# Layer 1 of experts 1 to 7 over two chunks of tokens at a time, and an earlier order of the first attention rounds

## The chip, the cores and the metric

The kernel runs on one core of one Trainium2 chip. The metric is the device time of one execution in microseconds. It was taken four times before the change: 698.27, 698.76, 696.95 and 697.79 us, median 698.03 us. The profile is of one execution, of 698.27 us.

Engines go by these names: PE multiplies matrices (PEld is its loading of the stationary operand), DVE, ACT and POOL work on vectors, SP only issues transfers. ACT and POOL issue transfers too. Each engine takes its instructions in the order of its own queue.

## The reference

Two parts, one behind the other: attention, whose output (reshaped) is the input x of a mixture of experts with a Sinkhorn weighting.

```python
# attention: batch 4, heads 8, sequence 768, head size 64
scores = scale * np.matmul(q, k.transpose(0, 1, 3, 2))
mask = np.where(is_retrieval, causal, causal & (is_sink | in_window))
a = softmax(np.where(mask, scores, -1e9))
x = np.matmul(a, v).transpose(0, 2, 1, 3).reshape(3072, 512)
# mixture: 8 experts, 512 -> 1024 -> 512
P = np.exp(x @ w_gate - max)
for _ in range(8):
    P /= P.sum(1, keepdims=True) + 1e-09
    P /= P.sum(0, keepdims=True) + 1e-09
    P *= N / E
for e in range(8):
    out += P[:, e:e + 1] * (np.maximum(x @ w1[e], 0.0) @ w2[e])
```

## The kernel before

**First phase, attention.** Work comes in units (batch b, 256 query rows g, four heads u). For each unit the keys and queries are transposed on PE (`emit_prep`, lines 271 and 277, with a DVE copy into kT at line 284), scores are made (`emit_scores`, line 476), ACT takes the exponential into PT (line 485), DVE masks PT (lines 494 and 497), PE multiplies with v (`gen_pv`, line 313), DVE normalizes into xn (lines 326 and 327), and PE and ACT turn the result into xT, the transposed x (`turn`, lines 342 and 345). Expert 0 is computed in between, as fillers (lines 383 and 397), as soon as 256 columns of xT are there. In the first batch, v arrives in another order of rows and is put in place by a small matmul against the identity (`gen_place_v`, line 136) and two copies, one by ACT (line 145) and one by DVE (line 143).

For PE, DVE and ACT the order of this phase is written out by hand. The first six rounds stand in the code one by one (lines 551 to 607); from the seventh on it is a loop. `warm(n)` issues n matmuls of 512 columns whose results nobody reads (line 299).

**Second phase.** Eight Sinkhorn steps on DVE with a tiny matmul each (line 645), and the rest of the fillers.

**Third phase, experts 1 to 7.** The 3072 tokens are six chunks of 512. The list `works` has 42 entries (expert e, chunk c). Both layers use a Strassen-Winograd scheme: each operand is cut into 2 x 2 blocks, seven products of blocks take the place of eight, and sums and differences of blocks are made beforehand on DVE (`left` for the stationary side, line 708, and `right` for the moving side, line 717), four per operand.

- `combine_w(e)` makes S1 from w1 and T2 from w2, `combine_x(c)` makes T1 from one chunk of x (cut into two halves of 256 tokens), `combine_h(e, c)` makes S2 from h.
- `layer1(e, c)` computes h for one chunk. The 1024 hidden features are cut into two halves of 512, and each half into two column groups g of 2 x 128. One product of one group is four matmuls of 256 moving columns (line 771) into a bank of PSUM. Several products are added up in the same bank "y", and between them ACT copies the bank to R (line 780). DVE adds R to another bank with a relu (line 786), and ACT ends the last block with a relu (line 810). There are four such banks.
- `layer2(e, c)` makes seven products of eight matmuls each (line 836), which are weighted with the gate and added to acc: products 1, 5, 6 and 7 by DVE (line 853), products 2, 3 and 4 by ACT into a tile (line 850) and an accumulating transfer issued by POOL (line 858). In the last two entries all are added by DVE.
- The first entry uses a plain layer 1 (`layer1_plain`, line 751: 32 matmuls of 512 columns), the last a plain layer 2 (`layer2_last`, line 888).

`body(n)` runs over the entries. In it, seven slots each issue two products of layer 1 for entry n and one product of layer 2 for entry n - 1, with the combinations of weights, x and h in given slots. At its end it makes the first two combinations of h for entry n. The order of DVE is by hand (line 943); that of PE, ACT, POOL and SP comes from a scheduler, from what the code emits. h lies in a pool of two buffers (line 743). The weights of the next expert are loaded at its predecessor's first chunk, w1 (line 157) and w2 (line 162) one after the other. Finished blocks are stored from SP's queue (line 822).

Of the kernel before, what the change touches and what calls it, by code (L numbers as in the profile page):

```python
# [3 lines left out]

# [6 lines left out]
F32 = mybir.dt.float32  # L11
# [25 lines left out]
def kernel(  # L37
# [88 lines left out]
    def place_v(g):  # L126
        run(gen_place_v(g), 2)

    def gen_place_v(g):

        parts = []
        for n in range(2):
            t = psA.tile([128, 512], F32, tag="mo", bufs=3, name=f"vp_{g}_{n}")
            rows = slice(64 * n, 64 * n + 64)
            for c in range(2):
                nc.tensor.matmul(
                    out=t[64 * c:64 * c + 64, :].rearrange("p (h d) -> p h d", h=H),
                    lhsT=ident16[rows, rows], rhs=vraw[g][rows, :, c, :], start=True, stop=True,
                )
            parts.append((v_tile(0)[:, :, 2 * g + n, 0:D], t.rearrange("p (h d) -> p h d", h=H)))  # L140
        for n, (dst, src) in enumerate(parts):
            if g == 2 or n:
                nc.vector.tensor_copy(out=dst, in_=src)
            else:
                nc.scalar.activation(out=dst, in_=src, func=AF.Copy, bias=0.0, scale=1.0)
            yield
# [403 lines left out]
    with tc.manual_schedule(engines=engines):  # L550
# [10 lines left out]
        make_masks((2,))  # L561
        emit_prep(*preps.pop())
        warm(2)
        soften(r0, (1,))
        r1 = scores(1)
        r1[0][0]()
        place = gen_place_v(0)
        run(place, 1)
        r1[1][0]()
        sum_later(0)  # L570
        emit_prep(*preps.pop())
        run(place, 1)
        finish_sums()
        make_masks((3,))
# [3 lines left out]
        place_v(1)  # L578
        turn()
        sum_later(1)  # L580
        r3 = scores(3)
        finish_sums(lambda: emit_prep(*preps.pop()))
# [3 lines left out]
        sum_later(2)  # L586
        r4 = scores(4)
        turn()
# [71 lines left out]

    CH = 512
# [58 lines left out]
    def combine_w(e):  # L720
        w1, w2 = expw[e]
        X = mp.tile([128, 4, 2, 512], F16, tag="S1", name=f"S1_{e}")
        yield from left(lefts1, e, [[w1[:, 2 * k:2 * k + 2, ts(i, 512)] for k in range(2)]
                                    for i in range(2)], [X[:, j] for j in range(4)])
        X = mp.tile([128, 4, 4, 256], F16, tag="T2", name=f"T2_{e}")
        yield from right(rights2, e, [[w2[:, 4 * k:4 * k + 4, ts(n, 256)] for n in range(2)]
                                      for k in range(2)], [X[:, j] for j in range(4)])

    def combine_x(c):
        X = mp.tile([128, 4, 2, 256], F16, tag=f"T1_{c}", bufs=1, name=f"T1_{c}")  # L730
        yield from right(rights1, c, [[xT[k][:, :, CH * c + 256 * n:CH * c + 256 * n + 256]
                                       for n in range(2)] for k in range(2)],
                         [X[:, j] for j in range(4)])

    def combine_h(e, c):
        h = hTs[e, c]
        X = [mp.tile([128, 2, 4, 128], F16, tag=f"S2{j}", bufs=1, name=f"S2{j}_{e}_{c}")
             for j in range(4)]
        yield from left(lefts2, (e, c), [[h[:, :, 4 * k:4 * k + 4, ts(i, 128)] for k in range(2)]
                                         for i in range(2)], X)  # L740

    def new_h(e, c):
        hTs[e, c] = mp.tile([128, 2, 8, 256], F16, tag="hT", name=f"hT_{e}_{c}")

    def layer1_plain(e, c):
        new_h(e, c)
        w1 = expw[e][0]
        for fb in range(8):
            l1 = psB.tile([128, CH], F32, tag="l1", name="l1b")
            for dc in range(4):  # L750
                nc.tensor.matmul(  # L751
                    out=l1, lhsT=w1[:, dc, ts(fb, 128)], rhs=xT[dc // 2][:, dc % 2, ts(c, CH)],
                    start=(dc == 0), stop=(dc == 3),
                )
            nc.scalar.activation(out=hTs[e, c][:, :, fb, :],
                                 in_=l1.rearrange("p (q m) -> p q m", q=2), func=AF.Relu,
                                 bias=0.0, scale=1.0)
            yield

    def layer1(e, c):  # L760

        new_h(e, c)
        h = hTs[e, c]
        banks, R = {}, {}

        def product(g, k, bank, first=False, last=False):
            if first:
                banks[g, bank] = psB.tile([128, 2, 256], F32, tag="l1", name=f"l1{bank}")
            for f in range(2):
                for dc in range(2):  # L770
                    nc.tensor.matmul(  # L771
                        out=banks[g, bank][:, f, :],
                        lhsT=lefts1[e][k - 1][:, dc, ts(2 * g + f, 128)],
                        rhs=rights1[c][k - 1][:, dc, :], start=(first and f == 0 and dc == 0),
                        stop=(last and f == 1 and dc == 1), skip_group_check=True,
                    )

        def copy(g, name, bank):
            R[name] = mp.tile([128, 2, 256], F32, tag=f"R{name}", bufs=1, name=f"R{name}")
            nc.scalar.activation(out=R[name], in_=banks[g, bank], func=AF.Copy, bias=0.0, scale=1.0)  # L780

        def block(g, i, n):
            return h[:, n, 4 * i + 2 * g:4 * i + 2 * g + 2, :]
# [43 lines left out]
    def layer2(e, c):  # L827
# [39 lines left out]
        for k in (1, 5, 6, 2, 7, 3, 4):  # L867
            bank, first, last, (i, n) = steps[k]
            product(k, bank, first, last)
            add(bank, i, n, k in (2, 3, 4) and (e, c) not in works[-2:])  # L870
# [5 lines left out]
    def layer2_last(e, c):  # L876


        h, w2 = hTs[e, c], expw[e][1]
        order = (4, 5, 0, 1, 2, 3, 6, 7)  # L880
        for q, i in ((0, 0), (0, 1), (1, 0), (1, 1)):
            pieces = 1 + (q == 1 and i == 1)
            for n in range(pieces):
# [3 lines left out]
                for j, f in enumerate(order):  # L887
                    nc.tensor.matmul(out=t, lhsT=h[:, q, f, ts(i, 128)],  # L888
                                     rhs=w2[:, f, n * width:(n + 1) * width],
                                     start=(j == 0), stop=(j == 7))  # L890
# [12 lines left out]

    gens = {name: iter(()) for name in ("l1", "l2", "h", "w", "x", "first")}
    gens["l1"] = layer1_plain(*works[0])
# [3 lines left out]

    def body(n):  # L910
        e, c = works[n]
        if c == 0 and e + 1 < E:
            expw[e + 1] = load_expert(e + 1)
        if c == 2 and e + 1 < E:
            gens["w"] = combine_w(e + 1)
        if e == LATE:
            gens["first"] = weight_first(c)
        if e == 1:
            gens["x"] = combine_x((c + 1) % NCH)
        for slot in range(7):  # L920
            if slot in (1, 2):
                go("first")
            go("l1", 2 if n == 0 and slot == 0 else 1)
            if slot in (1, 2):
                go("first")
            if slot in (1, 5):
                go("w")
                go("x", 2)
# [3 lines left out]
            if n == 0 and slot == 0:  # L932
                run(combine_w(1), 9)
                weigh_over()
        if n + 1 == len(works):
            gens["l2"] = layer2_last(e, c)
            return
        gens["h"] = combine_h(e, c)
        go("h", 2)
        gens["l2"] = layer2(e, c)  # L940
        gens["l1"] = layer1(*works[n + 1])

    with tc.manual_schedule(engines={mybir.EngineType.DVE}):
        for n in range(len(works)):
            body(n)
        go("l2", 9)

# [34 lines left out]
```

## Time and profile before

| | |
|---|---|
| median of four runs | 698.03 us |
| the profiled execution | 698.27 us |
| its span, first to last instruction | 696.4 us |
| first matmul of line 751 | 176.1 us |
| first and last layer-1 product (line 771) | 183.0 and 684.1 us |
| last DVE instruction | 692.3 us |
| PE busy in the span | 682.1 us |
| DVE busy | 575.9 us |
| ACT busy | 421.1 us |
| mean granted clock of PE | 0.991 |

The profile gives the span in microseconds from the first instruction. A group of instructions has a line of the kernel, an engine and an operation, out<-in by the program's names, shapes as partitions x elements, and a count. In the timeline a row has the start, the time it took (or the stretch of several merged instructions), and in brackets how long the engine had been idle and what released it. In the chain of waits a row has a start, a duration and the name. Matmuls are pipelined: a matmul's own duration (273 ns for 256 columns, 379 ns for 512) is longer than the distance between the starts of two of them.

### The profile page before, as it was taken

The page shows a single profiled execution, that of the slowest core. Times are in us where ns is not written, and L with a number is a line of the kernel's source. Part 1 is how long each engine was busy: PE and PEld are TensorE (multiplying, and loading weights), DVE is VectorE, ACT ScalarE, POOL GpSimd, SP SyncE. Part 2 cuts the span into 40 slices and gives each one's busy share as a digit, 9 for nine tenths or more (in the row PEclk, how much of TensorE's full clock was granted, in tenths as well). Part 3 has the DMA queues.
Part 4 walks back from the last instruction along what each step waited for, and adds up shares of the span by engine and source line. Part 5 has one row for each costly group of instructions (what it writes and reads, how often), then busy time and mean ns, then how long its engine had stood idle before and what let it go on. Part 6 is the DMA issues. An engine that isn't in the chain of part 4 may idle for free.

```text
span 696.4 us, 16654 instructions
## 1 busy us (share of the span) xinstructions
PE 682.1 (98%) x6751; PEld 568.3 (82%) x6751; DVE 575.9 (83%) x1165; ACT 421.1 (60%) x773; POOL 157.9 (23%) x183
## 2 busy tenths in 40 slices
PE   6999999999999999999999999999999999999997
PEld 3666666766688888888888888888888888888885
DVE  7886776757999988898898879988898888988785
ACT  5787777774565677775556554655556555555651
POOL 7443330000021131213112221222212212121220
PEclk7999999999999999999999999999999999999999
DMA  9999692000733396437834594349433954245676
GB/s 179 177 182 147 44 82 16 2 2 3 119 67 72 62 140 102 77 62 122 137 56 76 91 144 76 62 81 160 84 58 64 152 104 77 47 77 110 145 156 152
DMA packets 102686, 65.59 MB, mean 94 GB/s; under 512 B 66768, under 2 KB 83152, under 8 KB 102608
## 3 DMA queue, kind: packets, MB, share of 16 engines
q0 software_dynamic: 93408, 57.17, 60.9%
q1 hardware_dynamic: 7552, 6.30, 3.8%
q10 hardware_dynamic: 1648, 1.05, 0.5%
q8 instruction: 53, 0.87, 0.5%
q14 instruction: 25, 0.20, 0.1%
HBM read 52.45 MB, written 6.29 MB: 84 GB/s over the span
## 4 chain that ended last, share of the span: by engine, by line
PE 91%; ACT 3%; DMA 2%; DVE 2%; issue 1%; DVEq 0%; ACTq 0%
PE l1y L771 20%; PE l2y L836 20%; PE l2w L836 10%; PE l1w L771 10%; PE l L397 5%; PE l2z L836 5%; PE l1z L771 5%; PE l L383 5%; PE sc L476 3%; PE pv L313 3%; ACT PT L485 2%; DMA acc<-add 2%; PE tr L271 1%; PE last L888 1%; PE l1b L751 1%
## 5 line engine op out<-in xcount | busy, mean ns | idle before, releaser
L858 POOL DMA_DIRECT2D acc<-add x120 | 101.5, 846 | 379.8 <-ACT add L850 185.8
L771 PEld LDWEIGHTS <-S 128*128 128x128 f16 x1312 | 128.3, 98 | 15.7 <-issue 0.5
L836 PEld LDWEIGHTS <-S 128*128 128x128 f16 x1312 | 128.4, 98 | 14.9
L780 ACT ACTIVATE R<-l1y 128x512 f32<-128x512 f32 x164 | 98.1, 598 | 21.7 <-PE l1y L771 21.2
L771 PEld LDWEIGHTS <-w 128*128 128x128 f16 x984 | 96.2, 98 | 11.5
L836 PEld LDWEIGHTS <-hT 128*128 128x128 f16 x984 | 96.3, 98 | 11.1
L853 DVE SCALAR_TENSOR_TENSOR acc<-l2y,Pne,acc 128x256 f32<-128x256 f32 x212 | 92.5, 477 | 7.8 <-PE l2y L836 7.8
L771 PE MATMUL l1y<-T,S 128*128 128x256 f16 x656 | 98.4, 273 | 0.3 <-ACT R L780 0.3
L485 ACT ACTIVATE PT<-sc 128x1024 f16<-128x1024 f32 (+1 forms) x96 | 83.0, 922 | 15.1 <-PE sc L476 14.7
L836 PE MATMUL l2y<-T,S 128*128 128x256 f16 x656 | 85.0, 273 | 0.0
L850 ACT ACTIVATE add<-l2z,Pne 128x256 f32<-128x256 f32 x68 | 28.6, 471 | 74.1 <-PE l2z L836 74.1
L780 ACT ACTIVATE R<-l1w 128x512 f32<-128x512 f32 x82 | 49.0, 598 | 39.5 <-PE l1w L771 39.5
L708 DVE TENSOR_TENSOR S<-hT 128x1024 f16<-128x1024 f16 x82 | 56.3, 686 | 15.1 <-ACT hT L810 13.8
L786 DVE CUSTOM_DVE_ANT_0 hT<-l1z,R 128x512 f16<-128x512 f32 x82 | 56.6, 690 | 14.0 <-ACT R L780 13.8
L786 DVE CUSTOM_DVE_ANT_0 hT<-l1w,R 128x512 f16<-128x512 f32 x82 | 56.1, 684 | 7.7 <-PE l1w L771 7.7
L786 DVE CUSTOM_DVE_ANT_0 hT<-l1y,R 128x512 f16<-128x512 f32 x82 | 56.3, 687 | 4.4 <-ACT hT L810 0.5
L810 ACT ACTIVATE hT<-l1y 128x512 f16<-128x512 f32 x82 | 49.0, 597 | 17.2 <-PE l1y L771 15.9
L771 PE MATMUL l1y<-xT,w 128*128 128x256 f16 x328 | 49.2, 273 | 0.0
L771 PE MATMUL l1w<-xT,S 128*128 128x256 f16 x328 | 49.2, 273 | 0.0
L771 PE MATMUL l1z<-xT,w 128*128 128x256 f16 x328 | 49.2, 273 | 0.0
L771 PE MATMUL l1w<-T,S 128*128 128x256 f16 x328 | 49.2, 273 | 0.0
L771 PE MATMUL l1y<-T,w 128*128 128x256 f16 x328 | 49.2, 273 | 0.0
(120 smaller groups left out, 1058.8 us busy)
## 6 DMA issues: line engine op xcount, KB each, us to landing
acc<-add POOLq DMA_DIRECT2D x120, 256.0 KB, 3.3
w<-in_moe_w_dram POOLq DMA_DIRECT2D x16, 1024.0 KB, 10.8
out_dram<-acc SPq DMA_DIRECT2D x43, 128.0 KB, 2.4
k<-in_k_dram POOLq DMA_DIRECT2D x11, 256.0 KB, 10.9
q<-in_q_dram POOLq DMA_DIRECT2D x11, 256.0 KB, 11.4
v<-in_v_dram POOLq DMA_DIRECT2D x12, 192.0 KB, 11.5
acc<-in_v_dram POOLq DMA_DIRECT2D x3, 256.0 KB, 7.6
acc<-in_q_dram ACTq DMA_DIRECT2D x2, 256.0 KB, 5.3
```

Source lines behind the costliest of these rows:

```text
L383: nc.tensor.matmul(out=l1[:, ts(fb % 2, 256)], lhsT=w1[:, dc, ts(fb, 128)], rhs=xT[dc // 2][:, dc % 2, c0:c0 + 256], start=(dc == 0), stop ...
L397: nc.tensor.matmul(out=l2, lhsT=hT[fc // 2][:, o:o + 128], rhs=w2[:, fc, :], start=(fc == 0), stop=(fc == 7),)
L485: nc.scalar.activation(out=PT[:, :, c0:c0 + width], in_=sc[:, :, 0:width], func=AF.Exp, bias=0.0, scale=SCALE,)
L708: nc.vector.tensor_tensor(out=out_, in0=a_, in1=b_, op=op)
L771: nc.tensor.matmul(out=banks[g, bank][:, f, :], lhsT=lefts1[e][k - 1][:, dc, ts(2 * g + f, 128)], rhs=rights1[c][k - 1][:, dc, :], start=( ...
L780: nc.scalar.activation(out=R[name], in_=banks[g, bank], func=AF.Copy, bias=0.0, scale=1.0)
L786: nc.vector._custom_dve(TENSOR_ADD_SAT, out=block(g, i, n), in0=banks[g, bank], in1=R[name], s0=65504.0, s1=0.0)
L810: nc.scalar.activation(out=block(g, 1, 0), in_=banks[g, "y"], func=AF.Relu, bias=0.0, scale=1.0)
L836: nc.tensor.matmul(out=banks[bank][q], lhsT=lefts2[e, c][k - 1][:, q, f, :], rhs=rights2[e][k - 1][:, f, :], start=(first and q == 0 and f ...
L850: nc.scalar.activation(out=t[:, q, :], in_=banks[bank][q], func=AF.Copy, bias=0.0, scale=w)
L853: nc.vector.scalar_tensor_tensor(out=dst, in0=banks[bank][q], scalar=w, in1=dst, op0=ALU.mult, op1=ALU.add,)
L858: nc.gpsimd.dma_start(out=acc[c][:, i, n, :, :], in_=t, accum_op=ALU.add)
```

## The change

Two things are changed.

In the first phase, the rounds are in another order. Both copies of v's first two parts are on ACT; v is put in place ahead of the second scores (first part) and behind the fourth scores (second part); the last two masks are made earlier; two more `warm` matmuls stand behind the third scores; the second `turn` stands ahead of the fifth scores.

In the third phase, layer 1 takes two chunks of tokens (1024 tokens, a pair d) at a time and one half of the hidden features. The halves of tokens in the scheme are now the two chunks, so that one product of one group is two matmuls of 512 moving columns. The stationary blocks are 256 features wide, the halves of the FF dimension lying interleaved. An entry n of `works` computes (expert, pair c // 2, half c % 2), and layer 2 for a chunk follows when both halves of its pair are there: in `body(n)` it is that of entry n - 2. h lies in six tiles, handed round by name. The first half of the first pair is plain. w2 is loaded one chunk later than w1. In the first two entries, product 7 of layer 2 goes by transfer too. At the end, layer 2 of the last entry but one runs without a layer 1 beside it, between the first block of `layer2_last` and the others.

```diff
@@ first rounds @@
-        make_masks((2,))
+        make_masks((2, 3))
         emit_prep(*preps.pop())
         warm(2)
+        place_v(0)
         soften(r0, (1,))
+        sum_later(0)
         r1 = scores(1)
-        r1[0][0]()
-        place = gen_place_v(0)
-        run(place, 1)
-        r1[1][0]()
-        sum_later(0)
+        soften(r1, (0,))
         emit_prep(*preps.pop())
-        run(place, 1)
         finish_sums()
-        make_masks((3,))
         r2 = scores(2)
         soften(r1, (1,))
         soften(r2, (0,))
-        place_v(1)
+        warm(2)
         turn()
         sum_later(1)
         r3 = scores(3)
+        place_v(1)
         finish_sums(lambda: emit_prep(*preps.pop()))
...
         sum_later(2)
+        turn()
         r4 = scores(4)
-        turn()
@@ place_v @@
-            if g == 2 or n:
+            if g == 2:
                 nc.vector.tensor_copy(out=dst, in_=src)
             else:
                 nc.scalar.activation(out=dst, in_=src, func=AF.Copy, bias=0.0, scale=1.0)
@@ combinations @@
+        X = mp.tile([128, 4, 2, 2, 256], F16, tag="S1", name=f"S1_{e}")
+        w1 = w1.rearrange("p c (h i x) -> p c h i x", h=2, i=2)
+        yield from left(lefts1, e, [[w1[:, 2 * k:2 * k + 2, :, i, :] for k in range(2)]
                                     for i in range(2)], [X[:, j] for j in range(4)])
...
+    def combine_x(d):
+        X = mp.tile([128, 4, 2, 512], F16, tag=f"T1_{d}", bufs=1, name=f"T1_{d}")
+        yield from right(rights1, d, [[xT[k][:, :, ts(2 * d + n, CH)] for n in range(2)]
+                                      for k in range(2)], [X[:, j] for j in range(4)])
@@ h in six places @@
+    places = [mp.tile([128, 4, CH], F16, tag=f"hT{j}", bufs=1, name=f"hT{j}") for j in range(6)]
+    hold = {"now": places[0:2], "next": places[2:4], "second": places[4:6]}
+
+    def new_h(e, d, half):
+        for n in range(2):
+            hTs[e, 2 * d + n, half] = hold["second" if half else "now"][n]
+        if half:
+            two = [[hTs[e, 2 * d + n, k] for k in range(2)] for n in range(2)]
+            hold.update(now=hold["next"], next=two[1], second=two[0])
@@ layer1 @@
             if first:
-                banks[g, bank] = psB.tile([128, 2, 256], F32, tag="l1", name=f"l1{bank}")
-            for f in range(2):
-                for dc in range(2):
-                    nc.tensor.matmul(
-                        out=banks[g, bank][:, f, :],
-                        lhsT=lefts1[e][k - 1][:, dc, ts(2 * g + f, 128)],
-                        rhs=rights1[c][k - 1][:, dc, :], start=(first and f == 0 and dc == 0),
-                        stop=(last and f == 1 and dc == 1), skip_group_check=True,
-                    )
+                banks[g, bank] = psB.tile([128, CH], F32, tag="l1", name=f"l1{bank}")
+            for dc in range(2):
+                nc.tensor.matmul(
+                    out=banks[g, bank], lhsT=lefts1[e][k - 1][:, dc, half, ts(g, 128)],
+                    rhs=rights1[d][k - 1][:, dc, :], start=(first and dc == 0),
+                    stop=(last and dc == 1), skip_group_check=True,
+                )
@@ layer2 @@
-            add(bank, i, n, k in (2, 3, 4) and (e, c) not in works[-2:])
+            add(bank, i, n, k in ((2, 3, 4, 7) if (e, c) in works[:2] else (2, 3, 4))
+                and (e, c) not in works[-2:])
@@ the loop @@
+    early = {(1, 1): "w", (1, 4): "xx", (2, 0): "w", (2, 1): "x", (2, 3): "w", (2, 4): "x",
+             (3, 1): "wx", (3, 4): "x", (3, 5): "wx", (4, 1): "wx", (4, 5): "w"}
     def body(n):
         e, c = works[n]
         if c == 0 and e + 1 < E:
-            expw[e + 1] = load_expert(e + 1)
+            w1s[e + 1] = load_w1(e + 1)
+        if c == 1 and e + 1 < E:
+            expw[e + 1] = w1s.pop(e + 1), load_w2(e + 1)
         if c == 2 and e + 1 < E:
-            gens["w"] = combine_w(e + 1)
+            gens["w"] = chain(gens["w"], combine_w(e + 1))
...
+        if n == 0:
+            run(gens["l1"], 9)
+            run(combine_w1(1), 9)
+            run(combine_x(0), 9)
+            gens["w"], gens["x"] = combine_w2(1), combine_x(1)
+            go("w")
+            weigh_over()
+        if n == 3:
+            gens["x"] = combine_x(2)
         for slot in range(7):
...
-        gens["h"] = combine_h(e, c)
-        go("h", 2)
-        gens["l2"] = layer2(e, c)
-        gens["l1"] = layer1(*works[n + 1])
+        if n:
+            gens["h"] = combine_h(*works[n - 1])
+            go("h", 2)
+            gens["l2"] = layer2(*works[n - 1])
+        if n + 1 < len(works):
+            e, c = works[n + 1]
+            gens["l1"] = layer1(e, c // 2, c % 2)
...
+        go("h", 2)
+        last = layer2_last(*works[-1])
+        run(last, 1)
         go("l2", 9)
+        run(last, 9)
```

## The prediction

> **What bounds the kernel now.** First the page's head, then the stretches, then the chain of waits in order of time.
>
> ```profile
> span 696.4 us, 16654 instructions
> PE 682.1 (98%) x6751; PEld 568.3 (82%) x6751; DVE 575.9 (83%) x1165; ACT 421.1 (60%) x773; POOL 157.9 (23%) x183
> ```
>
> PE is busy 98% of the span, but its matmuls overlap, so the share says little. What one matmul costs is read where nothing waits:
>
> ```profile
> 10.00:20.00 10.00, 8.95 (x104) 5.30 (x102) 7.95 (x22) 6.64 (x10) 5.62 (x6) 0.56 1.48 196
> 400.00:500.00 100.00, 100.00 (x918) 89.63 (x917) 86.28 (x157) 55.90 (x115) 23.72 (x28) 1.00 0.62 102
> ```
>
> From 400 to 500 us 918 matmuls of 256 columns start in 100 us: 108.9 ns each. The start times of neighbours in the trace give 109.1 ns on average. The last three columns are granted clock, DMA share and GB/s: the clock is 0.56 from 10 to 20 us, 1.00 later.
>
> ```profile
> 15.55 0.60 PE pv L313 x8
> 16.15 0.86 PE sc L476 x8
> ...
> 176.24 6.92 PE l1b L751 x32
> ...
> 319.20 12.11 DMA acc<-add
> ```
>
> Line 751 runs 32 matmuls of 512 columns in 6.92 us: 216.25 ns each; by their start times, 215.7. So two matmuls of 256 take 218.2 ns and one of 512 takes 215.7 for the same columns. From 176 to 690 us I added up, over all neighbours, how much later a matmul starts than those two figures allow: 1.2 us in all. Layer 1 and layer 2 of experts 1 to 7 are one dense stream on PE; the other engines lie beside it. Only what shortens the stream, or opens a gap in it, counts.
>
> **Part 1, wider matmuls.** Layer 1 issues 41 x 56 = 2296 matmuls of 256 columns (the page's L771 groups: 656 and five of 328); the changed one issues 41 x 28 = 1148 of 512. 2296 x 109.1 ns = 250.5 us; 1148 x 215.7 ns = 247.6 us: -2.9 us. With 108.9 and 216.25 it is 250.0 - 248.3, -1.8; I keep -1.8 to -3.2 and take -2.9. Weight loads halve too, but each lies under a matmul (PEld, 98 ns) and gives nothing. [...]
>
> **Part 2, the start of expert 1.** Before, layer 1 of the second chunk runs beside layer 2 of the first at once. Now layer 2 starts a whole layer-1 half later, so PE has one half (28 matmuls, 6.0 us) almost alone, and its own chain shows: product, copy by ACT, next product into the same bank. The links are in the timeline:
>
> ```profile
> 183.00 0.60 PE L771 MATMUL l1y<-xT,w 128*128 128x256 f16 x4
> 183.70 0.60 ACT L780 ACTIVATE R<-l1y 128x512 f32<-128x512 f32 x1
> ...
> 185.17 0.68 DVE L786 CUSTOM_DVE_ANT_0 hT<-l1z,R 128x512 f16<-128x512 f32 x1
> ```
>
> ```profile
> 305.60 0.69 DVE L708 TENSOR_TENSOR S<-hT 128x1024 f16<-128x1024 f16 x1 [0.37 <-ACT hT L810]
> ```
>
> A copy starts 0.70 us after its product's first matmul (0.43 us of issue, 0.27 us to the end) and takes 0.60; a relu-sum on DVE takes 0.69, its successor starts 0.60 later; the h-combination waits for the last relu. I laid these on PE's built order from the moment line 751 ends (183.0, DVE done with its nine combinations of w1, x and w2 at about 182.1). PE then waits 0.07 us at product 7 of the first column group, 0.2 at product 5 of the second (of four "l1" banks one comes free only after a relu-sum), 0.16 at its product 3, 0.14 for the next half's second bank, 0.18 at its product 4, and 0.27 before layer 2's product 5, which needs the combination behind the last relu: 1.0 us. In the next body DVE still carries two w2 and two x combinations (4 x 0.60) on six relu-sums, four h-combinations and six additions (0.39 each): 10.8 us, of a body of 12.2, but started 1 us late, so that layer 2's product 7 and some banks wait another 0.6. Sum +1.6. Lower end +0.4: the built order already pulls the next half's products and layer 2's first product forward. Upper end +2.6: the body-2 waits come again in the third, where DVE has five combinations (11.4 us). The two extra accumulating transfers (line 858's kind) move 4 x 0.39 us from DVE to ACT, whose share is 60%.
>
> **Part 3, the end.** Layer 2 of the last chunk but one now has no layer 1 beside it. After the first output block of the last layer (8 x 0.216 us, which covers the combinations of h), seven products of 0.87 us are paced by DVE's additions: both halves 0.87 us, then 0.1 to the next product into the bank. Laid on the built order, PE waits 0.4 before product 6 (DVE still has four combinations and an output block), 0.13 before 7 and 0.15 before 4: +0.7 (0.2 to 1.4). Output blocks and tail are as now: eight stores more are in SP's queue then, at most 0.8 us each (SP's row issues 12 in 9.63 us from 677.9 on); they start some 7 us before the last block is ready and take 6.4.
>
> ```profile
> 685.17 7.09 PE L888 MATMUL last<-w,hT 128*128 128x512 f16 x40
> ...
> 692.30 0.48 DVE L893 SCALAR_TENSOR_TENSOR acc<-last,Pne,acc 128x256 f32<-128x256 f32 x1 [0.39 <-PE last L888]
> ```
>
> **Part 4, the first rounds.** Now the second v copy is DVE's, behind a kT copy, and the first pv waits until 15.55; the third scores start at 16.08. With both v copies on ACT and the placing moved ahead of the second scores: two more mask operations delay the second kT by 0.63 us (scores at 12.4 instead of 11.8), but pv follows the transposes at 14.2 and the third scores start at about 15.1, 1.0 us sooner. Then 0.8 us is given back: two more dense matmuls (0.85 us at the half clock), and the two v copies of the next group stand in ACT's queue ahead of the fourth scores' exponentials, whose successors PE and DVE wait for. At the first filler (22.6 us) I get -0.2. POOL's reloads follow these releases and move with them. Where the clock comes up one stretch sooner, I get -1.0; where ACT's queue costs a whole v copy more, +0.8.
>
> **Part 5, weights.** w2 of the next expert is loaded a chunk later, so the two transfers of 11 us no longer follow one another. In the row at 319.20 an addition took 12.11 us to land behind them, and PE lost 0.5 us at 332.2, the one large gap. -0.3 (0 to -0.5). POOL's additions behind the w2 load wait as they do now, for the last chunk's layer 2.
>
> DVE's x-combinations (24 of 512 elements, 0.34 each, become 12 of 1024, 0.60 each) and the six places for h cost nothing: from expert 2 on DVE needs some 10.3 us in 12.2. If that cover went, a combination would cost PE 0.6 us each.
>
> **Sum.** -2.9 + 1.6 + 0.7 - 0.2 - 0.3 = -1.1 us. The profiled execution took 698.27 us, 1.9 around its span of 696.4; it is 0.24 above the median of 698.03. I put the same difference on the median: 696.9 us.
>
> **Rivals.**
> First, the seams close: the early pulled products fill both seams (start 0.4, end 0.2). -2.9 + 0.4 + 0.2 - 0.2 - 0.3 = -2.8, 695.2 us. For it: the built order interleaves just there. Against it: the last relu, the combination and product 5 stay one chain.
>
> Second, slower: in every body one product of layer 1 waits for the copy into its bank. Two wide matmuls last 0.431 us where four narrow ones lasted 0.436, so that each cover shrinks. The price is in the trace: four times PE lost 0.09 to 0.1 us before such a product. 41 x 0.097 = +4.0, in all +2.9, 700.9 us; it decides from 0.027 us per body (1.1 / 41). Against it: 37 of 41 bodies show no such gap, and the order of products is the same.
>
> Third, the clock: at 0.5 from 8.5 to 18.8 us. If a first-rounds gap keeps it there for longer, say a third of that stretch more (3.4 us), PE loses up to 1.7: 696.9 + 1.7 = 698.6 us. Against it: the new order has fewer gaps between 12 and 15.4 us. [...]
>
> Fourth, it saves nothing: 512 columns behind each other with weights of different places cost 218 ns; the 2.9 us vanish, +1.8, 699.8 us. Against it: lines 397 and 888 show 216 ns too.
>
> **How the numbers follow.** Forecast 0.55, its own range 695.9 to 697.9; first rival 0.22, second 0.10, third 0.08, fourth 0.05. 0.2% is 1.4 us, about what a measurement of this kernel tells from no change: faster means under 696.6. Some 0.20 of the forecast's 0.55 lies there; with the first rival 0.42. Slower (over 699.4): 0.10 + 0.05 = 0.15. The same: 0.43. The range, 695.0 to 699.2, takes in the first rival and the third and leaves out the second and fourth.
>
> **What would show it.** Layer-1 matmuls 215.7 ns apart and 1148 of them; gaps of about 1 us in PE between 183 and 195 us, 0.6 in the next 12, 0.7 after the last layer-1 product, none between; the third scores near 15.1 us, line 751's matmuls within 1 us of 176.1. Gaps in every body, or a first l1b over 1 us off, would prove me wrong.

## The result, and the profile after

The changed kernel takes 697.21 us, the median of 34 runs (696.38 to 698.22). The kernel before takes 697.99 in the 56 runs made by then (696.55 to 700.76). The ratio is 0.9988, 95% interval 0.9982 to 0.9994: 0.8 us less, real but small, within the 0.2% that the prediction called the same. The forecast was 696.9. The profiled execution of the changed kernel took 697.16 us, close to the median. Its parts need not be typical, as the first rounds and the tail show below.

The head of its page, to be held against the one of before:

```profile
span 695.5 us, 14325 instructions
PE 678.8 (98%) x5605; PEld 455.0 (65%) x5605; DVE 572.3 (82%) x1147; ACT 422.2 (61%) x779; POOL 159.6 (23%) x185
```

There are 1146 fewer matmuls in the records, and the weight loads lost 113 us of busy time; the span lost 0.9 us. Four moments, read from the two timelines, say where this one microsecond comes from in these two executions (us):

| | before | after | difference |
|---|---|---|---|
| first filler matmul (`l`) | 22.63 | 20.97 | -1.66 |
| first matmul of `l1b` | 176.10 | 174.43 | -1.67 |
| from there to the end of the last DVE instruction | 516.68 | 515.03 | -1.65 |
| from there to the end of the span | 3.57 | 5.99 | +2.42 |
| span | 696.35 | 695.46 | -0.90 |

Two stretches won 1.7 us each, and the last few microseconds gave 2.4 back. Not all of it is the change's. In the middle 0.5 us is one gap of the kernel before, at 332.2 us, which two other profiles with the old layer 1 don't have: they take 516.1 and 516.2 us for this stretch (the new rounds alone, and more to do in PE's gap, both below). At the front a part hangs on where the clock's stretches happened to lie (half clock from 8.54 to 18.78 us before, from 9.03 to 12.45 after).

The dense middle, as stretches (length, then busy time and count of PE, PEld, DVE, ACT and POOL, then clock, DMA share, GB/s):

```profile
10.00:20.00 10.00, 8.49 (x114) 4.98 (x113) 8.45 (x24) 8.53 (x14) 5.62 (x6) 0.88 1.47 197
400.00:500.00 100.00, 100.00 (x694) 67.81 (x693) 88.19 (x161) 55.24 (x113) 22.86 (x27) 1.00 0.58 96
```

In 100 us 694 matmuls start instead of 918, PE being as full as before. The next matmul starts 216.2 ns after one of 512 columns in layer 1 on average, the waits at the seams included. In the first row the clock from 10 to 20 us is 0.88; before it was 0.56.

The seam at the start of expert 1, in PE's timeline (start, length, and in brackets how long PE stood still and what ended it):

```profile
191.08 1.05 PE L845 MATMUL l2w<-T,S 128*128 128x256 f16 x8
...
197.16 1.05 PE L845 MATMUL l2y<-T,S 128*128 128x256 f16 x8 [0.17 <-DVE S L701]
198.47 0.59 PE L781 MATMUL l1w<-xT,S 128*128 128x512 f16 x2 [0.26 <-ACT R L789]
```

and the chain of waits at the same place:

```profile
189.07 0.60 PE l1y L781 x2
189.70 0.61 ACT hT L819
190.33 0.70 DVE S L701
191.06 0.69 DVE S L701
...
197.10 0.61 DVE hT L795
...
197.82 0.60 ACT R L789
...
198.47 0.59 PE l1w L781 x2
```

This is the predicted chain: the relu, the combination of h, product 5 of layer 2; and in the next body product 7 behind a combination, then a layer-1 product behind a copy which itself waited for DVE's relu-sum. Counted over all neighbours, a PE gap being what a start comes later than 215.7 or 109.1 ns allow, they are 0.14, 0.14, 0.18, 0.17, 0.08, 0.33 and 0.43 us between 184 and 199 us: 1.47 us.

The other seam, after the last layer-1 product, in PE's timeline:

```profile
679.35 1.03 PE L845 MATMUL l2y<-T,S 128*128 128x256 f16 x8 [0.22 <-DVE acc L862]
...
684.22 4.72 PE L897 MATMUL last<-w,hT 128*128 128x512 f16 x29
```

It costs 0.47 us (0.39 at this product, which is number 6, and 0.04 and 0.05 at two others). What follows is the part that the prediction had at nothing. SP's queue over the end, all of it (a row's length is from its first issue to the end of its last), and DVE's last instruction:

```profile
679.81 1.25 SPq L831 DMA_DIRECT2D out_dram<-acc  x2
681.16 0.60 SPq L907 DMA_DIRECT2D out_dram<-acc  x1
681.87 8.38 SPq L831 DMA_DIRECT2D out_dram<-acc  x10
690.35 2.66 SPq L907 DMA_DIRECT2D out_dram<-acc  x4
```

```profile
688.98 0.48 DVE L902 SCALAR_TENSOR_TENSOR acc<-last,Pne,acc 128x256 f32<-128x256 f32 x1 [0.39 <-PE last L897]
```

Line 831 stores the last chunk but one and the one before it, line 907 the last chunk. The last chunk's pieces are ready at 686.25, 687.98, 688.59 and 689.46; ACT sends its halves of them from 686.29 on. SP sends its halves from 690.35 on, in a burst that ends at 693.01, since ten stores of other chunks stand ahead. At 0.66 us from one to the next ten would need 6.6 us, but they took 8.38: some held SP for longer than the usual 0.60 us, one for 1.71. Why these did is not shown. In the kernel before SP sent each piece 0.02 to 0.12 us after it was ready, the last at 692.81.

The first rounds, in PE's timeline:

```profile
13.53 0.54 PE L308 MATMUL pv<-v,PT 128*128 128x65 f16 x12
14.38 0.39 PE L471 MATMUL sc<-kT,kT 64*128 64x256 f16 x4 [0.32 <-DVE kT L279]
...
20.97 1.03 PE L378 MATMUL l<-xT,w 128*128 128x256 f16 x8
```

The third scores start 1.70 us sooner than before, and the first filler still 1.66 sooner: nothing is given back between. In this execution the full clock came at 12.45 us. Three other profiles with the new rounds (narrow matmuls, without the second warm pair, the changed kernel again) have it at 14.35 to 15.37 us, and there the third scores stand at 15.12 or 15.13 and the first filler at 21.69 to 21.79: 0.95 and about 0.9 us sooner than before.

### The profile page after: what moved, and what is told of

The parts are those of the page before. It is cut to its first block, busy times and chain, and to the rows that moved or that the text cites. A ratio compares the mean times of both kernels' runs of the same rounds, so it can differ in the third digit from the quotient of the medians.

```text
span 695.5 us, 14325 instructions
## 1 busy us (share of the span) xinstructions
PE 678.8 (98%) x5605; PEld 455.0 (65%) x5605; DVE 572.3 (82%) x1147; ACT 422.2 (61%) x779; POOL 159.6 (23%) x185
## 3 DMA queue, kind: packets, MB, share of 16 engines
q10 hardware_dynamic: 1648, 1.05, 0.6%
## 4 chain that ended last, share of the span: by engine, by line
PE 90%; ACT 4%; DVE 3%; issue 1%; DMA 1%; ACTq 0%; DVEq 0%
PE l1y L781 20%; PE l2y L845 20%; PE l2w L845 10%; PE l1w L781 10%; PE l L392 5%; PE l1z L781 5%; PE l2z L845 5%; PE l L378 5%; PE sc L471 3%; PE pv L308 3%; ACT PT L480 3%; PE tr L266 1%; PE l1b L762 1%; PE last L897 1%; PE xt L337 1%
## 5 line engine op out<-in xcount | busy, mean ns | idle before, releaser
L867 POOL DMA_DIRECT2D acc<-add x122 | 103.1, 845 | 382.3 <-DVE hT L795 192.9
L845 PEld LDWEIGHTS <-S 128*128 128x128 f16 x1312 | 128.2, 98 | 50.0 <-DVE S L701 0.9
L781 PE MATMUL l1y<-T,S 128*128 128x512 f16 x328 | 97.7, 379 | 0.0
L781 PEld LDWEIGHTS <-S 128*128 128x128 f16 x656 | 64.2, 98 | 44.2 <-issue 1.2
L781 PEld LDWEIGHTS <-w 128*128 128x128 f16 x492 | 48.1, 98 | 32.5 <-issue 0.2
L781 PE MATMUL l1w<-xT,S 128*128 128x512 f16 x164 | 48.9, 379 | 0.3 <-ACT R L789 0.3
L781 PE MATMUL l1z<-xT,w 128*128 128x512 f16 x164 | 48.9, 379 | 0.0
L781 PE MATMUL l1y<-T,w 128*128 128x512 f16 x164 | 48.8, 379 | 0.0
L781 PE MATMUL l1w<-T,S 128*128 128x512 f16 x164 | 48.8, 379 | 0.0
L781 PE MATMUL l1y<-xT,w 128*128 128x512 f16 x164 | 48.8, 379 | 0.0
L378 PE MATMUL l<-xT,w 128*128 128x256 f16 x384 | 48.0, 272 | 0.1
```

The costliest lines, as they stand in the source:

```text
L378: nc.tensor.matmul(out=l1[:, ts(fb % 2, 256)], lhsT=w1[:, dc, ts(fb, 128)], rhs=xT[dc // 2][:, dc % 2, c0:c0 + 256], start=(dc == 0), stop ...
L781: nc.tensor.matmul(out=banks[g, bank], lhsT=lefts1[e][k - 1][:, dc, half, ts(g, 128)], rhs=rights1[d][k - 1][:, dc, :], start=(first and d ...
L845: nc.tensor.matmul(out=banks[bank][q], lhsT=lefts2[e, c][k - 1][:, q, f, :], rhs=rights2[e][k - 1][:, f, :], start=(first and q == 0 and f ...
L867: nc.gpsimd.dma_start(out=acc[c][:, i, n, :, :], in_=t, accum_op=ALU.add)
```

## The experiments

The kernel before ran beside each group of experiments: median 698.23 (22 runs) with the first four, 698.20 (29) with the next four, 697.96 (15) with the last two. Ratios are against these.

**The old first rounds in the changed kernel.** The rounds' order and `place_v` are put back; the wide layer 1 stays.

```diff
-        place_v(0)
         soften(r0, (1,))
-        sum_later(0)
         r1 = scores(1)
-        soften(r1, (0,))
+        r1[0][0]()
+        place = gen_place_v(0)
+        run(place, 1)
+        r1[1][0]()
+        sum_later(0)
         emit_prep(*preps.pop())
+        run(place, 1)
...
-        warm(2)
+        place_v(1)
         turn()
```

> The changed kernel with the first rounds of before. Theory: in the profile the new rounds bring line 751's kind of matmul 1.66 us earlier (174.44 us instead of 176.10), so this one should start it near 176.1 again, with the clock at half until about 18.8 us, and take about 1.7 us more than the changed kernel: about 698.9 us, slower than before too. Rival (my prediction's -0.2): the two orders are worth the same and the 1.66 us are the chance of where the clock's window fell in one execution; then about 697.4 us.

Measured: 698.36 us (12 runs), ratio 1.0003 (0.9992 to 1.0014), 0.5 us under the theory. The wide layer 1 by itself wins nothing that can be measured. Its stretch from 10 to 20 us:

```profile
10.00:20.00 10.00, 8.37 (x98) 5.08 (x96) 7.79 (x21) 7.05 (x11) 5.63 (x6) 0.67 1.48 196
```

98 matmuls instead of 114 and a clock of 0.67 instead of 0.88: the rounds are those of before, and the first filler starts at 23.04. So what the front wins comes from the rounds and not from the wide layer 1. How much of it is their order and how much the clock this profile doesn't tell, since here the clock was at half twice, from 7.75 to 14.58 and again from 17.99 to 24.82 us.

**The new first rounds in the kernel before.** The opposite: layer 1 narrow as before, the rounds as in the change.

```diff
-        r1 = scores(1)
-        r1[0][0]()
-        place = gen_place_v(0)
-        run(place, 1)
-        r1[1][0]()
         sum_later(0)
+        r1 = scores(1)
+        soften(r1, (0,))
...
-        place_v(1)
+        warm(2)
         turn()
```

> The kernel before with the first rounds of the change and nothing else of it. Theory: the same 1.7 us from the other side: about 696.3 us, faster than the whole change (697.2), which would then be all in the rounds, with the wide layer 1 giving back what it wins. Rival: 697.8 us.

Measured: 696.46 us (10 runs, 695.77 to 696.82), ratio 0.9975 (0.9965 to 0.9985), 1.75 us less. By the medians the small part of the change alone wins more than the whole change; the two intervals overlap.

```profile
10.00:20.00 10.00, 8.46 (x114) 4.89 (x114) 8.42 (x23) 8.53 (x14) 5.75 (x6) 0.89 1.48 197
175.00:690.00 515.00, 514.87 (x4662) 455.81 (x4660) 451.11 (x844) 299.22 (x600) 109.96 (x130) 1.00 0.56 97
```

The first row is nearly that of the changed kernel, the second a full PE with narrow matmuls. Both loads of the next expert's weights stand where they stood before, and yet the gap of 0.5 us that the profile of before had at 332.2 us is not there.

**The stores of the last chunk but one on two queues.** In the changed kernel, one half of them is issued by ACT.

```diff
-            nc.sync.dma_start(
+            (nc.scalar if o and c == NCH - 2 else nc.sync).dma_start(
```

> The changed kernel with half of the eight stores of the last chunk but one issued from ACT instead of SP. Theory: after the last DVE instruction 6.0 us pass in the changed kernel and 3.6 in the one before, because the last block's stores queue in SP behind these eight; with four of them gone the stretch falls to 3.6 to 4.2 us and the time to about 695.1 us. Rival: the transfers themselves are at their rate (200 to 300 GB/s in the last 6 us) and the stretch stays at 5.5 to 6 us: 697 us.

Measured: 695.63 us (6 runs, 695.28 to 696.19), ratio 0.9966 (0.9953 to 0.9980), 1.6 us under the changed kernel (1.2 under its later runs, below). SP's queue, and then ACT's:

```profile
...
682.53 4.12 SPq L831 DMA_DIRECT2D out_dram<-acc  x6
687.01 3.70 SPq L907 DMA_DIRECT2D out_dram<-acc  x4
```

```profile
682.84 3.85 ACTq L831 DMA_DIRECT2D out_dram<-acc  x4
687.01 3.91 ACTq L907 DMA_DIRECT2D out_dram<-acc  x4
```

SP is through with the other chunks at 686.65, and both queues start the last chunk at 687.01, when its next piece is there (DVE ends it at 686.98). From the last DVE instruction (690.19) to the end are 4.1 us, not 6.0, as the theory had it. So the end of the changed kernel was set by SP's queue.

**Narrow matmuls in the changed kernel.** Each matmul of 512 columns becomes two of 256, each with its own load of the same weights; all else is the change's.

```diff
-            for dc in range(2):
-                nc.tensor.matmul(
-                    out=banks[g, bank], lhsT=lefts1[e][k - 1][:, dc, half, ts(g, 128)],
-                    rhs=rights1[d][k - 1][:, dc, :], start=(first and dc == 0),
...
+            for f in range(2):
+                for dc in range(2):
+                    nc.tensor.matmul(
+                        out=banks[g, bank][:, ts(f, 256)],
+                        lhsT=lefts1[e][k - 1][:, dc, half, ts(g, 128)],
+                        rhs=rights1[d][k - 1][:, dc, ts(f, 256)],
...
```

> The changed kernel with each layer-1 matmul of 512 columns of experts 1 to 7 issued as two of 256, all else the same. Theory: 1148 x (218.2 - 215.7 ns) = +2.9 us, about 700.1 us, and matmuls 109 ns apart. Rival: the weight loads had a share as well, and the loss is larger than 3.5 us; or the gaps swallow it and it is under 1.5 us.

Measured: 700.49 us (5 runs, 700.34 to 700.69), ratio 1.0036 (1.0023 to 1.0049). Against the changed kernel's 0.9988 that is 0.0048 of 698: 3.3 us, give or take about 1. The profiles tell it closer: from the first `l1b` to the last DVE instruction it takes 518.2 us against 515.0, 3.2 us more. Of these 2.9 are the matmuls themselves, as the sum said (by their starts, waits left out, 109.2 ns at 256 columns and 215.8 at 512); about 0.3 are larger gaps.

```profile
400.00:500.00 100.00, 100.00 (x919) 89.64 (x917) 86.88 (x160) 55.99 (x115) 23.06 (x28) 1.00 0.60 99
```

**Both seams mended, with the stores on two queues.** Besides the edit of the stores: expert 1's w2 and x combinations are made ahead of the point where DVE becomes short, and the last free layer-2 product is pulled ahead of the h-combinations.

```diff
-    early = {(1, 1): "w", (1, 4): "xx", (2, 0): "w", (2, 1): "x", (2, 3): "w", (2, 4): "x",
+    early = {(1, 1): "w", (1, 4): "xx", (2, 3): "w", (2, 4): "x",
...
-            go("w")
+            go("w", 2)
+            go("x")
             weigh_over()
...
+        go("l2", 1)
         go("h", 2)
```

> The changed kernel with three repairs: half of the last chunk but one's stores from ACT (as in the run with two queues, 695.6 us); at the start of expert 1 one w2 and one x combination moved from the second body to before the first, where DVE idles 2.1 us; at the end layer 2's first product and its additions ahead of two of the four h-combinations and of the first output block. Theory: the waits of 0.33 and 0.43 us in the second body and of 0.39 us at the end are DVE's order; two of the three go and the rest of the start (0.6 us, the chain of copies) stays, so that the gaps above 60 ns after 183 us fall from 2.0 us to about 1.0 and the time to 694.6 us. Rival: the waits only move to the next product, and the time is that of the two queues, 695.6 us.

Measured: 695.29 us (6 runs, 694.70 to 695.77), ratio 0.9958 (0.9943 to 0.9972), the lowest of all. The gaps at the start are 0.14, 0.14, 0.18, 0.18 and 0.08 us, the end's are 0.25 together: of 1.94 us 0.98 is gone. Where product 7 and the copy held PE up, nothing does now:

```profile
196.86 0.49 PE L845 MATMUL l2y<-w,hT 128*128 128x256 f16 x3
197.26 0.59 PE L781 MATMUL l1w<-xT,S 128*128 128x512 f16 x2
```

By the medians this is 0.34 us under the version with the stores alone, between theory and rival, and the intervals overlap. In the profile the tail is not 4.1 us but 5.4. SP's queue at the end, and its longest wait there (us, times, longest):

```profile
682.84 5.29 SPq L831 DMA_DIRECT2D out_dram<-acc  x4
688.22 2.70 SPq L907 DMA_DIRECT2D out_dram<-acc  x4
```

```profile
SPq L831 <- DMA out_dram<-acc: 2.4, 1, 2.4
```

Ahead of the last of the four stores SP waits 2.4 us until an earlier store of the output has landed. With the stores on two queues the time to issue them is no longer the only thing that can hold SP up.

**More to do for PE in the gap of the old rounds.** In the kernel before, three matmuls of 512 columns that nothing reads are put where PE waits for the second v copy. They don't move the order; whether they do something to the clock is what the run is to show.

```diff
         run(place, 1)
+        t = psA.tile([128, 512], F32, tag="mo", bufs=3, name="warm")
+        for _ in range(3):
+            nc.tensor.matmul(out=t, lhsT=ident16, rhs=kTs[units[0]].rearrange("p a s -> p (a s)"),
+                             start=True, stop=True)
         finish_sums()
```

> The kernel before with three matmuls of 512 columns, read by nobody, in PE's gap from 14.3 to 15.55 us ahead of the first pv, its rounds otherwise as they were. Theory A (the clock): what the new rounds win is that PE has no such gap and the clock is granted earlier; then this wins most of it, about 697.0 us, with mean clocks of the runs at 0.994 and above. Theory B (the order): the new rounds win by pv no longer waiting for DVE's copy and the third scores coming 1.7 us earlier; then this wins under 0.5 us: 697.8 us or more.

Measured: 697.72 us (12 runs), ratio 0.9993 (0.9985 to 1.0002); the mean granted clock of its runs is 0.994 or more in all of them, where that of the kernel before goes down to 0.988.

```profile
10.00:20.00 10.00, 8.69 (x109) 5.03 (x105) 7.88 (x22) 7.07 (x11) 5.63 (x6) 0.79 1.48 198
```

```profile
16.08 0.39 PE L476 MATMUL sc<-kT,kT 64*128 64x256 f16 x4
```

The third scores stand at 16.08 as before, the first filler at 22.58 instead of 22.63, and about 0.5 us is won by the medians, less than the measurement tells apart. The full clock came at 14.20 us, before the first of the three starts (14.29), so that they didn't bring it. They may have kept it: of the 3.4 us from 14.20 on PE is busy for 2.63 and the clock stays, while the old rounds without them (the first experiment) have PE busy for 1.96 of the 3.4 us from 14.58 on, and half clock follows. A better clock alone gives at most a part of the 1.75 us.

**Without the second warm pair.** The change's `warm(2)` behind the third scores is taken out.

```diff
         soften(r2, (0,))
-        warm(2)
         turn()
```

> The changed kernel without the two matmuls that nobody reads behind the third scores. Theory A: they help to keep the clock; without them its runs show mean clocks under 0.993 more often and it takes 0.5 to 1.5 us more, 698 us. Theory B: the clock is granted at 12.4 us, before they start (15.3 us), and they only fill a wait: 697.2 us, the same.

Measured: 697.16 us (12 runs), ratio 0.9986 (0.9977 to 0.9995): the same as with it, within what the runs tell apart. In its profile the third scores start at 15.12 and the first filler at 21.79, against 15.13 and 21.69 in the changed kernel run again. No cost of the pair is to be seen, and no gain beyond 0.1 us.

**The changed kernel again**, unedited, beside these.

> The changed kernel itself on the chip of these runs, for comparison with them: 697.2 us, 0.8 us under the kernel before.

Measured: 696.86 us (12 runs), ratio 0.9988 (0.9978 to 0.9998). In its profile DVE ends at 690.19 and the span at 695.40: a tail of 5.2 us, with the same ten stores ahead of the last four on SP:

```profile
682.59 7.72 SPq L831 DMA_DIRECT2D out_dram<-acc  x10
690.40 2.58 SPq L907 DMA_DIRECT2D out_dram<-acc  x4
```

Here everything up to the last DVE instruction is 0.73 us later than in the first profile, and yet SP's queue ends at the same time (692.98 and 693.01), so that the tail of 6.0 is at the long end. This profile is also the better partner for the one with two queues: the first `l1b` (175.16) and the last DVE instruction (690.19) stand at the same moments in both, and the tail is 5.2 us in one and 4.1 in the other. There, 1.1 us are the stores' alone.

**The seams alone**, the stores left on SP.

```diff
-            go("w")
+            go("w", 2)
+            go("x")
             weigh_over()
...
+        go("l2", 1)
         go("h", 2)
```

> The changed kernel with the repairs at the start of expert 1 and at the end of layer 2, and its stores all in SP's queue as in the change. The seams repaired save 1.1 us up to the last DVE instruction (513.9 us from line 762's first matmul, against 515.0). Theory: the last stores are set by SP's queue, which starts no earlier than the stores before allow, so that the half of it won at the end is lost in the tail: 0.5 us under the change, about 696.4 us, with 6 us or more after the last DVE instruction. Rival: all of it arrives, 695.8 us.

Measured: 697.23 us (11 runs), ratio 0.9989 (0.9979 to 0.9998): no gain over the changed kernel, and less than both theory and rival had. (This run and the next are from another chip than the others, so their ratios are compared.) In its profile the stretch from the first `l1b` to the last DVE instruction is 513.9 us instead of 515.0, so the seams did close. SP's queue:

```profile
...
682.73 6.42 SPq L831 DMA_DIRECT2D out_dram<-acc  x8
689.25 2.62 SPq L907 DMA_DIRECT2D out_dram<-acc  x4
```

The eight stores of the last chunk but one begin at 682.73, where they begin at 683.22 in the changed kernel. DVE ends at 688.34, the queue at 691.87. In this execution all of the gain arrives: the queue and the span end 1.1 us sooner than in the changed kernel's first profile (693.01 and 695.46), with the same front and the same tail of 6.0. But at 696.33 us it is the quickest of the eleven, and the median shows none of the 1.1 us. A part, 0.2 us, lies outside the span: these runs take 1.9 to 2.0 us more than their spans, the changed kernel's 1.7 to 1.9. What took the rest isn't known; that SP's queue swallows it, as the theory had it, is not shown.

**One accumulating transfer less near the end.** On top of the best version, product 4 of the third entry from the end is added by DVE, so that SP's first late store needn't wait for a transfer to land.

```diff
-                and (e, c) not in works[-2:])
+                and (e, c) not in works[-2:] and not (k == 4 and (e, c) == works[-3]))
```

> The run with seams and tail repaired (695.3 us), and the last addition of the chunk before (product 4 of the third entry from the end) by DVE instead of by an accumulating transfer, for whose landing SP's queue waits at 680.8 us. Theory: SP's queue is the limit; its stores start 1 us sooner and the stretch after the last DVE instruction falls from 5.4 to about 4 us: 694.3 us. Rival: the transfers are at their rate (about 280 KB per us from 683 to 687 us), and it stays within 0.3 us of 695.3.

Measured: 695.67 us (5 runs, 694.92 to 696.51), ratio 0.9964 (0.9951 to 0.9976). No gain over 695.29 by the median, and the rival is as near as the theory is far. The profile says otherwise: SP's late stores start 1.0 us sooner than in the best version, the tail is 4.1 us instead of 5.4, both as the theory had it, and the span is 692.2 us instead of 693.8.

```profile
681.80 3.84 SPq L831 DMA_DIRECT2D out_dram<-acc  x4
```

But the spans of the other four runs are 693.6 to 693.8 us. Whether the landing is what was left of the tail stays open.

## Why the prediction was near, point by point

The total was right (-1.1 foreseen, -0.8 measured), but two of its steps were wrong by one to two us each, in opposite directions. That they cancelled is luck. The terms, in us:

| step | predicted | measured | from |
|---|---|---|---|
| wide matmuls | -2.9 | -2.9 to -3.2 (medians -3.3, about 1 either way) | narrow matmuls put back |
| start of expert 1 | +1.6 | +1.47 | gaps in PE |
| end, layer 2 alone | +0.7 | +0.47 | gaps in PE |
| tail and stores | 0 | +1.1 to +2.4 | two queues; the profiles |
| first rounds | -0.2 | -1.75 (-1.05 to -2.44) | new rounds alone |
| w2 loaded later | -0.3 | 0 | gap absent without it |

**Wide matmuls: right.** 2 x 109.2 against 215.8 ns held for 1148 matmuls with weights of two places, and so the fourth rival (it saves nothing) falls.

**Seams: right in mechanism and nearly in size.** Working out DVE's and ACT's queues against PE's built order found the waits and their products, and 1.6 us where 1.47 were measured; by bodies it is 1.0 and 0.6 against 0.71 and 0.76, so a part of the agreement is chance. At the end the wait before product 6 came as foreseen (0.4 against 0.39), the two smaller ones only to a third. The first rival (the seams close by themselves) falls: they closed only when combinations were moved. So does the second (a wait in every body): from 199 us up to the last seam there are 0.4 us of gaps in all, the largest of 0.11.

**The tail: the step that failed.** The prediction said: "Output blocks and tail are as now: eight stores more are in SP's queue then", which "start some 7 us before the last block is ready and take 6.4". Their length was nearly right (8 in 6.42 us with the seams mended, 7.0 in the changed kernel), the conclusion was not, for three reasons that the timeline shows. Two stores of an earlier chunk stand in the same burst. The eight begin only at 683.22, 6.2 us before the last DVE instruction ends. And the last chunk's own SP stores were left out: its first pieces are ready 3.2 us before the last one, and while the eight are being issued they pile up behind them; four at 0.66 us are 2.66 us after 690.35. In the kernel before only one of them was left at that moment. How long SP is held by one store is seen in its row for line 831 (issues, least, median and longest time in ns, first and last start):

```profile
L831 SPq DMA_DIRECT2D out_dram<-acc x13: 596/601/1708, 676.0 to 689.2; - x13
...
DMA to landing us min/median/max: 2.0/2.7/4.4
```

0.60 us each, and 128 KB each: at that pace about 0.2 MB per us leaves through SP. Put on two queues, 1.6 us came back in the median and 1.1 in the tails of two profiles that are alike up to the last DVE instruction, which shows the cause. One store holds SP for 0.60 us of the 2.7 that it takes to land, but that time adds up: ten of them one behind the other took 8.38 us of SP's queue in the changed kernel, and that is the bound at the end. With two queues SP issued six in 4.12 us while ACT issued four in 3.85.

**The first rounds: mechanism right, one term of the sum wrong.** The step had the third scores near 15.1, 1.0 us sooner, and then "0.8 us is given back" by the two warm matmuls and by v copies ahead of the exponentials. The first half came true: 15.12 or 15.13 in the three profiles with the later clock. The second did not: the warm pair shows no cost, and what the third scores win is still there at the first filler, but for about 0.1 (0.95 and about 0.9 us there, 1.70 and 1.66 in the first profile).

How much is the rounds' own and how much the clock's? In the kernel before and in the changed kernel without the second warm pair half clock begins at the same moment, 8.54 us. Before, it lasts until 18.78, there until 15.37, and the first filler stands at 22.63 and at 21.79: 0.84 us for the new rounds together with a clock that is up 3.41 us sooner there. That is close to the prediction's -1.0 for a clock that comes up one stretch sooner. The other 0.8 of the first pair goes with stretches that lie 0.5 us later (half clock from 9.03 to 12.45) and is, as far as these profiles tell, a chance of the execution. Why the medians show 1.75, more than 0.84, is not settled; their interval reaches down to 1.05. The third rival (the clock stays half for longer) is not borne out for the new order: half clock lasted 3.4 us in the changed kernel and 6.8 when it was run again, against 10.2 in the kernel before and twice 6.8 in the first experiment. That a gap of PE keeps the clock down was the author's estimate; the run with more matmuls in PE's gap fits it (mean clock 0.994 or more, where it goes down to 0.988 without them), and no run shows more.

**The later load of w2: not borne out.** The 0.5 us at 332.2 us was one execution's. Two profiles with the old loading (the new rounds alone, more to do in PE's gap) don't have it.

**What stays open.** The new rounds alone (0.9975) and the wide layer 1 alone (1.0003) would make 0.9978 together; the whole change has 0.9988. The intervals allow both, so no further interaction is claimed. That mended seams are worth their 1.1 us isn't shown by the medians, neither with all stores on SP (no gain) nor with two queues (0.34 us, within the noise), though two profiles have it up to the last DVE instruction and one of them up to the end. What sets the end once the stores are on two queues, the landings that SP waits for or the transfers themselves, was not separated. Nor was the kernel before run with its late stores on two queues and the new rounds, so that the wide layer 1 isn't shown to pay against that.

## What to carry to other kernels

Follow the last output to the end of the span: list the stores in each queue with their issue times, the last block's own among them, before a change upstream is counted as won; what is won ahead of a full store queue need not come out (here 0.73 us at the front of one execution did not, and of the seams' 1.1 us the median shows nothing). When one change holds two parts, price and run each alone: here the reordered rounds, a term of -0.2 in the working, were by the medians worth more than the whole, and the wide layer 1, the main part, won nothing by itself. With the stores on two queues and the seams mended the whole takes 695.29 us, 0.9958 of the kernel before; its interval (0.9943 to 0.9972) still touches that of the rounds alone (0.9965 to 0.9985). A total that comes out right shows nothing of its terms.

## What was not expected of the hardware

The length of the half-clock stretch at the start changes from run to run of one and the same kernel. In the profiles it was about 3.4, 6.8 or 10.2 us long, once, twice or three times the shortest (9.03 to 12.45 in the changed kernel, 7.53 to 14.35 when it was run again, 8.54 to 18.78 in the kernel before); the first experiment has two of 6.8. Its length goes with where it begins. In the five profiles where it begins at 8.73 us or later (all with the new rounds) PE is busy for 2.9 to 3.3 of its first 3.4 us, and the full clock follows. In the six where it begins at 8.54 us or earlier PE is busy for 2.5 to 2.8 of them, and half clock goes on. Over the 66 runs of the kernel before, time and mean granted clock go together (correlation -0.71): 697.26 us in the 31 runs at 0.997 or above, 698.66 in the 26 below 0.993. That spread of 1.4 us is larger than the change measured here, so runs have to be many and side by side. The mean clock of a single run is a rough sign only. It counts half clock behind the last matmul too (1.7 us of the span in the kernel before, 3.8 in the changed one). And a trace can lack the first stretch: the profile with two queues has no clock on record before 14.05 us, though its two matmuls of 512 columns at 11.00 took 1.06 us together, as long as the two at half clock in the changed kernel. What sets the three lengths no run shows.
